# Six planner times and two copy engines changed in a sliding-window attention + gated MLP kernel

## The chip, the cores and the metric

The kernel runs on one core of one Trainium2 chip. The metric is the device time of one execution in microseconds (us), as the median of several runs. The profile shows one such execution. TensorE is called PE below (its weight loads PEld), VectorE DVE, ScalarE ACT, GpSimd POOL, SyncE SP.

## The reference

Eight batches `b` of eight heads, 576 positions, head size 64. Each query sees itself and the 63 keys before it. What follows is an MLP over 4608 rows of 512 columns with 2048 hidden columns, whose activation is `h * cos(h)`.

```python
scores = scale * np.matmul(q, k.transpose(0, 1, 3, 2))
mask = (rel >= 0) & (rel < window)          # window = 64
attn = softmax(np.where(mask, scores, -1e9))
x = np.matmul(attn, v).transpose(0, 2, 1, 3).reshape(B * S, H * D)
h = x @ w_in
out = (h * np.cos(h)) @ w_out
```

## The kernel before, in words

**Tiles.** The 4608 rows are cut into nine tiles `mt` of 512 rows, a batch into nine blocks `j` of 64 positions, the heads into four pairs `p`. A unit is one block of one pair: 64 queries against 128 keys, for two heads.

**The MLP of a tile.** PE makes `h_ps` in 16 blocks (`first`, L437; four matmuls each, one for each pair's quarter `ks` of xT), ACT takes the sine (L594), DVE multiplies (L597), and PE makes `out_ps` from the result (L609), 64 matmuls in four row groups. Each row group's `out_ps` is copied to `out_sb`, by DVE for even and by ACT for odd groups (L613). Before the 16 blocks `skewed` does the first three blocks by quarters, so that quarter 0 of xT is enough to begin with.

**Attention of batch b = t + 1** is done in the stage `t`, mostly among the output matmuls of tile `mt = t`. Units are put in groups of up to four, numbered here by `i` within the stage. A group goes through: scores on PE (`g_scores_across`, matmul L301), mask and maximum on DVE (`g_max`, L325, one instruction for each unit), exponentials with their sum on ACT (`g_exp`, L336), reciprocal on DVE (`g_inv`, L343), product on POOL (`g_norm`, L350; for the first three groups of stage 0 on DVE), and a transpose (`g_trans`). The transpose is a DMA on SP's queue (L362), except for the groups in `DIRECT` of stage 0 (i = 0 to 3, 8 and 9), where PE transposes (L359) and DVE copies the result (`g_put`). Then `values` multiplies with v on PE (L377) into `o_ps`, for the four pairs in turn, and `put_x` copies `o_ps` into xT (L113, the line of a helper that all copies share).

**Loads.** q, k and v of later batches are loaded by DMAs that POOL issues (`load_chunk`, L161, five chunks of 128 positions for q and five for k; `load_v`, L167). For batches from 2 on SP transposes q and k by DMA (`turn`, L246).

**What sets the order.** Nothing reorders at run time: each engine works its instructions in the order in which the code emits them. From stage 0's second half on, that order comes from a plan. `at(time, fn, ...)` (L461) books a step at a planner time; `pump(time)` (L464) emits all steps booked up to that time; the MLP loops call `pump` once after each `h_ps` block (planner time +1) and once after each four output matmuls (+1). A stage is `T = 32` planner units long, and its output matmuls begin at `Q = 16`. So a booked time says between which matmuls a step stands in PE's order, and where it stands on every other engine and queue. It says nothing of microseconds.

**Banks.** Scores go into PSUM banks by a list: in stage 0 two groups at a time over the banks X1, S, X0 in turn (L479); in later stages in two bursts, the groups i = 0 to 3 (banks t, t, t, X1) and, at i = 4, all others (t, t, t, S, X1, X0), L481. A bank is written again only when `g_max` has read it.

**The end of a stage.** The last group of a stage gets its reciprocal, product and transpose by times set from the stage's end (`lags`, L482: `T - 0.79`). The four `values` steps are booked at 1.01 before the next tile (L518), and the four copies into xT at 0.81, 0.71, 0.61 and 0.51 before it (L523). So DVE's order there is: copy of pair 0, the last reciprocal, copies of pairs 2 and 3; ACT copies pair 1.

Of the kernel before, what the change touches and what calls it, by code (L numbers as in the profile page):

```python
# [39 lines left out]
Q = 16  # L40
T = 2 * Q
LAGS = (0.2, 1, 3.2, 3.4, 3.8)
# [18 lines left out]
def kernel(  # L61
# [209 lines left out]
    groups = [[(0, p, j) for j in range(GF * g, GF * g + GF)] for p in range(PAIRS) for g in range(TU // GF)]  # L271
# [12 lines left out]
    direct = set(range(n_first)) | {n_first + i for i in DIRECT}  # L284
# [176 lines left out]
    def at(time, fn, *args):  # L461
        plan.append((time, len(plan), fn, args))
# [8 lines left out]
    ready = {(0, p, j): 0 for p in range(PAIRS) for j in range(TU)}  # L471
    n = n_first
    for t in range(B - 1):
        last = max(i for i, units in enumerate(groups) if units[0][0] == t + 1)
        time = T * t + Q - 1.4
        for i in range(last + 1 - n):
            time += PACE * len(groups[n - 1]) if i else 0
            if t == 0 and i % 2 == 0:
                at(time, g_scores_across, n, 2, (S_BANKS + S_BANKS)[i % 3:])  # L479
            elif t and i in (0, 4):  # L480
                at(time, g_scores_across, n, last + 1 - n if i else 4, "t t t S X1 X0".split() if i else "t t t X1".split())  # L481
            lags = LAGS[:2] + tuple(T * t + T - 0.79 - time + 0.01 * s for s in range(3)) if n == last and t else LAGS  # L482
            for lag, fn in zip(lags, (g_max, g_exp, g_inv, g_norm)):
                at(time + lag, fn, n, *("d" for _ in range(1) if fn is g_norm and n < n_first + 3))
            at(time + (4.6 if n in direct else lags[-1]), g_trans, n)
            if n in direct:
                at(time + 4.9, g_put, n)
            ready.update({unit: time + (5.9 if n in direct else 8.5) for unit in groups[n]})
            n += 1

    for b in range(1, B):
        t0 = T * (b - 1)
        if b == 1:
            for p in range(0, PAIRS, 2):
                for i, (tr, put) in enumerate(((tr_q, put_q), (tr_k, put_k))):
                    at(7 + 1.8 * (p + i), tr, b, p, p + 1)
                    for e, engine in enumerate("da"):
                        at(7.01 + 1.8 * (p + i) + 0.01 * e, put, b, p + e, engine)
        else:
            for i, name in enumerate(("q", "k")):  # L500
                for c in range(NC):
                    time = 4 + 0.5 * (c + NC * i) if b == 2 else t0 - T + 8 + 0.9 * (c + NC * i)
                    at(t0 - T + (22.1 if b == 2 else 18.5) + 1.44 * (c - 2) if i and c > 1 else time, load_chunk, name, b, c)
                for c, (lo, hi) in enumerate(((0, 2), (2, NC)) if i else ((0, NC),)):
                    at(t0 - (5.8 if b > 2 else 3.4) + 0.1 * i + 0.1 * c, turn, name, b, lo, hi)
            for c in range(5):
                at(t0 + 3.5 + 0.9 * c, load_v, b, c)
            for time, part in ((13.5, 0), (19.9, 2), (21.7, 3)):
                at(t0 + time, spread_v, b, part, None)
# [5 lines left out]
    for mt in range(1, n_mt):  # L515
        for p in range(PAIRS):
            time = max(ready[b, p - p % 2 + i // TU, j] for i in range(2 * TU) for b, j in (divmod(mt * TU + i % TU, NU),))
            time = max(time, 25.5) if mt == 1 else T * mt - (8.01 if mt == n_mt - 1 else 1.01)  # L518
            at(time, values, mt, p)
            if mt == 1:  # L520
                at(time + 0.3 + 0.2 * (p % 2), put_x, mt, p)
            else:
                at(time + 0.2 + 0.1 * p, put_x, mt, p, "a" if p == 1 else None)  # L523


    for name in ("q", "k"):
# [122 lines left out]
```

## Time and profile before

| | |
|---|---|
| median of 3 runs | 311.13 us (309.15, 311.13, 311.28) |
| the profiled execution's own time | 309.06 us |
| its span, first to last instruction | 307.1 us |
| PE busy | 292.3 us, 95% of the span |
| ACT busy | 235.6 us, 77% |
| DVE busy | 222.9 us, 73% |
| POOL busy | 170.3 us, 55% |

Times inside the profile run from the span's start. Stage 0's attention lies at about 41 to 60 us, and a later stage takes some 31 us: about 14 us of `h_ps` blocks, then about 17 us of output matmuls with the attention of the next batch. A timeline row has the start, the time from the first start to the last end of the merged instructions, the engine and line, the operation, the tiles written and read, and their count; what stands in square brackets is the idle time of the engine before the row, and what ended it. A matmul's row ends when its pipeline is empty, so the next matmul can begin before that end.

### The profile page before, as it was taken

How to read it: one execution, taken by the hardware profiler on the slowest of the kernel's cores; microseconds unless marked ns; L12 is line 12 of the kernel's file. 1: busy time of each engine (PE TensorE's matmuls, PEld its weight loads, DVE VectorE, ACT ScalarE, POOL GpSimd, SP SyncE). 2: the span in 40 equal slices, each digit the busy share in tenths (PEclk: the TensorE clock that was granted, in tenths of full speed). 3: DMA queues.
4: the chain of work that ended last, by engine and by line, in shares of the span. 5: the costliest groups of instructions: out<-in, count | busy, mean ns of one | idle time of the engine just before them, and what ended most of it. 6: DMA issues, size and time to landing. Idle time of an engine off the chain costs nothing.

```text
span 307.1 us, 8045 instructions
## 1 busy us (share of the span) xinstructions
PE 292.3 (95%) x2732; PEld 148.6 (48%) x2732; DVE 222.9 (73%) x841; ACT 235.6 (77%) x785; POOL 170.3 (55%) x204
## 2 busy tenths in 40 slices
PE   3979999899989989999989999999999999999996
PEld 2658854444444444444444545454544454454443
DVE  4866998778957896789867986798689768235801
ACT  4898799767997799779976998699869986116600
POOL 8997357793789376946895489648803620000000
PEclk9979999999999999999999999999999999999999
DMA  7999999999999999999999999999994342011011
GB/s 143 180 211 209 206 160 154 122 166 146 224 114 153 151 229 147 152 135 229 149 164 149 215 159 162 159 208 174 176 174 149 78 101 99 0 70 69 2 68 69
DMA packets 168921, 44.73 MB, mean 146 GB/s; under 512 B 158000, under 2 KB 164144, under 8 KB 168880
## 3 DMA queue, kind: packets, MB, share of 16 engines
q0 software_dynamic: 99344, 18.06, 82.6%
q1 hardware_dynamic: 69392, 25.96, 46.2%
q8 instruction: 21, 0.34, 0.5%
q10 hardware_dynamic: 144, 0.20, 0.2%
q14 instruction: 20, 0.16, 0.2%
HBM read 36.70 MB, written 9.44 MB: 150 GB/s over the span
## 4 chain that ended last, share of the span: by engine, by line
PE 57%; DVE 11%; DMA 9%; ACT 7%; POOL 6%; issue 5%; SPq 3%; DVEq 0%; POOLq 0%
PE h_ps L437 30%; PE out_ps L609 15%; DMA wT<-w 8%; DVE s L325 5%; PE h_ps L414 5%; ACT e L336 5%; POOL w L350 4%; SPq L246 2%; PE o_ps L377 2%; DMA q<-in_q_dram 2%; DVE v L113 2%; PE s_ps L301 1%; SPq L362 1%; PE out_ps L449 1%; POOL k L161 1%
## 5 line engine op out<-in xcount | busy, mean ns | idle before, releaser
L609 PE MATMUL out_ps<-w_out,gT 128*128 128x512 bf16 x560 | 125.2, 380 | 0.0
L437 PE MATMUL h_ps<-xT,w_in 128*128 128x512 bf16 x512 | 112.5, 379 | 0.6 <-ACT xT L113 0.5
L597 DVE TENSOR_TENSOR gT<-h_ps,sin 128x512 bf16<-128x512 f32 x128 | 84.8, 687 | 30.6 <-ACT sin L594 30.6
L350 POOL TENSOR_TENSOR w<-e,rden 128x512 bf16<-128x512 f32 (+1 forms) x76 | 72.0, 960 | 55.5 <-DVE rden L343 43.6
L336 ACT ACTIVATE e<-s,negm 128x128 f32<-128x128 f32 x256 | 98.6, 387 | 0.3 <-DVE negm L325 0.3
L594 ACT ACTIVATE sin<-h_ps 128x512 f32<-128x512 f32 x128 | 73.8, 599 | 31.5 <-PE h_ps L437 30.8
L609 PEld LDWEIGHTS <-gT 128*128 128x128 bf16 x560 | 53.0, 98 | 62.4
L437 PEld LDWEIGHTS <-w_in 128*128 128x128 bf16 x512 | 49.6, 98 | 60.2 <-issue 1.4
L325 DVE CUSTOM_DVE_ANT_0 s<-s_ps,mask 128x128 f32<-128x128 f32 x256 | 57.8, 280 | 1.7 <-PE s_ps L301 1.5
L336 ACT ACTIVATION_READ_ACCUMULATOR e<-s,negm 128x1 f32 x256 | 47.9, 187 | 0.0
L167 POOL DMA_DIRECT2D v<-in_v_dram x40 | 34.1, 873 | 1.0 <-DMA k<-in_k_dram 1.0
L161 POOL DMA_DIRECT2D k<-in_k_dram x30 | 26.4, 883 | 10.5 <-DMA v<-in_v_dram 9.0
L161 POOL DMA_DIRECT2D q<-in_q_dram x30 | 25.4, 883 | 10.0 <-DMA w_out<-in_moe_w_out_dram 8.6
L113 ACT COPY out_sb<-out_ps 128x512 f32<-128x512 f32 (+1 forms) x18 | 10.1, 562 | 26.1 <-PE out_ps L609 20.6
L113 DVE CAST xT<-o_ps 128x512 bf16<-128x512 f32 x26 | 16.9, 681 | 12.5 <-PE o_ps L377 11.0
L113 DVE COPY out_sb<-out_ps 128x512 f32<-128x512 f32 x18 | 12.2, 679 | 13.2 <-PE out_ps L609 13.2
L343 DVE RECIPROCAL rden<-den 128x4 f32<-128x4 f32 (+1 forms) x80 | 13.5, 171 | 10.6 <-ACT e L336 6.1
L325 DVE DVE_READ_ACCUMULATOR2_ANT negm<- 128x1 f32 x256 | 20.4, 80 | 0.0
L414 PE MATMUL h_ps<-xT,w_in 128*128 128x256 bf16 x128 | 16.4, 283 | 0.0
L113 DVE COPY v<-v 64x1024 bf16<-64x1024 bf16 (+1 forms) x19 | 15.7, 824 | 0.4
L414 PEld LDWEIGHTS <-w_in 128*128 128x128 bf16 x128 | 12.4, 102 | 1.8
L425 DVE TENSOR_TENSOR gT<-h_ps,sin 128x512 bf16<-128x512 f32 x16 | 10.8, 688 | 3.0 <-ACT sin L420 2.9
(60 smaller groups left out, 182.0 us busy)
## 6 DMA issues: line engine op xcount, KB each, us to landing
out_dram<-out_sb SPq DMA_DIRECT2D x16, 512.0 KB, 7.5
v<-in_v_dram POOLq DMA_DIRECT2D x32, 128.0 KB, 6.6
q<-in_q_dram POOLq DMA_DIRECT2D x24, 128.0 KB, 11.1
k<-in_k_dram POOLq DMA_DIRECT2D x24, 128.0 KB, 8.4
w_out<-in_moe_w_out_dram POOLq DMA_DIRECT2D x2, 1024.0 KB, 17.0
w_in<-in_moe_w_in_dram POOLq DMA_DIRECT2D x2, 768.0 KB, 11.1
wT<-w SPq DMA_TRANSPOSE x66, 5.7
out_dram<-out_sb SPq DMA_DIRECT2D x3, 256.0 KB, 2.0
```

What stands on the lines that cost most here:

```text
L113: {"a": nc.scalar.copy, "p": nc.gpsimd.tensor_copy}.get(engine, nc.vector.tensor_copy)(out, in_)
L161: nc.gpsimd.dma_start(out=st[name, b][:n, c].rearrange("p (h d) -> p h d", h=H), in_=src.rearrange("h p d -> p h d"))
L167: nc.gpsimd.dma_start(out=vt.rearrange("p (h d) -> p h d", h=H), in_=v[b, :, c * 128:c * 128 + n, :].rearrange("h p d -> p h d"))
L325: nc.vector.tensor_tensor_reduce(out=s[:, u], in0=s_ps[:, u], in1=mask[:, 2 - j % 2 if j else 0], scale=-scale if b else -1.0, scalar=BIG, ...
L336: nc.scalar.activation(e[:, u], s[:, u], AF.Exp, bias=negm[:, u:u + 1], scale=1.0 if n < n_first else -1.0, accum_out=den[:, u:u + 1])
L343: nc.vector.reciprocal(out=rden[:, 0:len(groups[n])], in_=den[:, 0:len(groups[n])])
L350: (nc.gpsimd if engine == "p" else nc.vector).tensor_tensor(out=w[:, 0:u], in0=e[:, 0:u], op=ALU.mult, in1=rden[:, 0:u].unsqueeze(2).to_br ...
L414: nc.tensor.matmul(out=st["h0", i][:, e], lhsT=w_in_sb[:, ks, ff * 128:ff * 128 + 128], rhs=st["xT", 0][:, ks, half], start=ks + e == 0, s ...
L437: nc.tensor.matmul(out=st["h", ff], lhsT=w_in_sb[:, ks, ff * 128:ff * 128 + 128], rhs=st["xT", mt][:, ks], start=start, stop=stop)
L594: nc.scalar.activation(sin, h_ps, AF.Sin, bias=math.pi / 2.0)
L597: nc.vector.tensor_tensor(out=gt[:, e], in0=h_ps, in1=sin, op=ALU.mult)
L609: nc.tensor.matmul(out=o_ps[e], lhsT=gT[ff // 2][:, ff % 2, ms * 128:ms * 128 + 128], rhs=w_out_sb[:, ff], start=ff == 0, stop=ff == n_ff - 1)
```

## The change

Four places change. (1) In stage 0, the PE transposes of group i = 3 are booked at +5.5 instead of +4.6, and their copy 0.3 behind them. (2) For batch 2, the loads of k chunks 2 and 3 are booked with those of chunks 0 and 1 (planner times 7.5 and 8.0 instead of 22.1 and 23.5), and chunk 4 at 26.9 instead of 25.0. (3) In the stages from 1 on, the second burst of scores is booked no earlier than `Q + 4.3` after the stage's begin; all later groups of the stage move with it. By the list of groups this moves a burst in stage 2 alone (by 1.4 units); elsewhere it lies at Q + 4.36 already. (4) At the end of the stages from 1 on, the last group's reciprocal, product and transpose are booked at `T - 0.65`, and ACT copies pair 2 of xT instead of pair 1.

In the emitted order this reads as follows. PE, stage 0: the 12 score matmuls of groups 8 and 9 and four output matmuls now stand ahead of the three transposes of group 3. DVE there: the reciprocal of group 5 and the mask steps of group 8 stand ahead of the copy of group 3. POOL there: four k loads in a row, the products of groups 3 to 7, the last k load, the other products. PE, stage 2: eight output matmuls ahead of the burst of 48 score matmuls. DVE and ACT there: the mask steps of group 4 stand behind a v copy and two reciprocals, and ACT copies `out_sb` behind group 4's exponentials instead of group 5's. At the ends of six stages DVE's order is: copies of pairs 0 and 1, the last reciprocal, copy of pair 3. SP in stage 2: the DMA transpose of group 6 stands behind the three DMA transposes of batch 4's q and k (`turn`) instead of ahead of them. No instruction is added or removed; elsewhere POOL's and SP's orders are the same.

```diff
+            if t and i == 4:
+                time = max(time, T * t + Q + 4.3)
...
-            lags = LAGS[:2] + tuple(T * t + T - 0.79 - time + 0.01 * s for s in range(3)) if n == last and t else LAGS
+            lags = LAGS[:2] + tuple(T * t + T - 0.65 - time + 0.01 * s for s in range(3)) if n == last and t else LAGS
...
-            at(time + (4.6 if n in direct else lags[-1]), g_trans, n)
+            lag = (5.5 if i == 3 else 4.6) if n in direct else lags[-1]
+            at(time + lag, g_trans, n)
             if n in direct:
-                at(time + 4.9, g_put, n)
-            ready.update({unit: time + (5.9 if n in direct else 8.5) for unit in groups[n]})
+                at(time + lag + 0.3, g_put, n)
+            ready.update({unit: time + (lag + 1.3 if n in direct else 8.5) for unit in groups[n]})
...
-                    at(t0 - T + (22.1 if b == 2 else 18.5) + 1.44 * (c - 2) if i and c > 1 else time, load_chunk, name, b, c)
+                    if i and c > (3 if b == 2 else 1):
+                        time = 26.9 if b == 2 else t0 - T + 18.5 + 1.44 * (c - 2)
+                    at(time, load_chunk, name, b, c)
...
-                at(time + 0.2 + 0.1 * p, put_x, mt, p, "a" if p == 1 else None)
+                at(time + 0.2 + 0.1 * p, put_x, mt, p, "a" if p == 2 else None)
```

## The prediction

> **What bounds the kernel now.** I read the page first: how busy the engines are, and the mean pace of PE.
>
> ```profile
> span 307.1 us, 8045 instructions
> PE 292.3 (95%) x2732; PEld 148.6 (48%) x2732; DVE 222.9 (73%) x841; ACT 235.6 (77%) x785; POOL 170.3 (55%) x204
> L437 PE MATMUL h_ps<-xT,w_in 128*128 128x512 bf16 x512 | 112.5, 379 | 0.6 <-ACT xT L113 0.5
> ```
>
> PE is the bound, with few gaps; the change removes no work, so it can gain only what PE waits. One row takes 379 ns from start to end, but 512 of them fill 112.5 us, so PE takes up a new one each 0.22 us. A waiting PE therefore loses some 0.16 us more than the idle time in brackets says, and I count each wait from the 0.22.
>
> Then the view of waits, PE's rows:
>
> ```profile
> PE tw_ps L359 <- POOL w L350: 2.8, 3, 1.1
> PE o_ps L377 <- DMA wT<-w: 2.2, 2, 1.2
> PE s_ps L301 <- DVE negm L325: 0.8, 1, 0.8
> PE h_ps L437 <- ACT xT L113: 0.5, 2, 0.2
> ```
>
> The columns are total, times, longest. Behind the start-up, these are about all of PE's waits. The edits are aimed at the first (of its three, two lie in stage 0's attention), the third and the fourth; the second, for DMA transposes, is touched by none, and it is where a wait may move to.
>
> **Edits 1 and 2, stage 0.** PE's timeline from 42 to 62 us, then POOL's, then two DVE rows:
>
> ```profile
> 48.36 1.03 PE L609 MATMUL out_ps<-w_out,gT 128*128 128x512 bf16 x4
> 50.13 0.34 PE L359 MATMUL tw_ps<-ident,w 128*128 128x128 bf16 x3 [0.74 <-POOL w L350]
> 50.40 0.36 PE L301 MATMUL s_ps<-kT,qT 64*64 64x128 bf16 x12
> 50.69 2.77 PE L609 MATMUL out_ps<-w_out,gT 128*128 128x512 bf16 x12
> 53.39 0.42 PE L301 MATMUL s_ps<-kT,qT 64*64 64x128 bf16 x16
> 53.74 1.90 PE L609 MATMUL out_ps<-w_out,gT 128*128 128x512 bf16 x8
> 56.68 0.34 PE L359 MATMUL tw_ps<-ident,w 128*128 128x128 bf16 x3 [1.04 <-POOL w L350]
> 57.81 0.70 PE L377 MATMUL o_ps<-wT,v 128*64 128x64 bf16 x32
> 60.22 0.70 PE L377 MATMUL o_ps<-wT,v 128*64 128x64 bf16 x32
> ```
>
> ```profile
> 45.35 1.79 POOL L161 DMA_DIRECT2D k<-in_k_dram  x2
> 49.25 0.82 POOL L350 TENSOR_TENSOR w<-e,rden 128x384 bf16<-128x384 f32 x1 [2.11 <-DVE negm L325]
> 50.98 0.84 POOL L350 TENSOR_TENSOR w<-e,rden 128x384 bf16<-128x384 f32 x1
> 51.75 0.94 POOL L161 DMA_DIRECT2D k<-in_k_dram  x1
> 53.49 0.73 POOL L161 DMA_DIRECT2D k<-in_k_dram  x1
> 54.23 3.19 POOL L350 TENSOR_TENSOR w<-e,rden 128x384 bf16<-128x384 f32 x4
> ```
>
> ```profile
> 49.39 0.28 DVE L325 CUSTOM_DVE_ANT_0 s<-s_ps,mask 128x128 f32<-128x128 f32 x1
> 54.69 0.17 DVE L343 RECIPROCAL rden<-den 128x3 f32<-128x3 f32 x1
> ```
>
> PE is through at 48.36 + 4 x 0.22 = 49.24 and starts group 3's transposes at 50.13: 0.89 lost. After the edit 12 score matmuls come first. They aren't free to go at once: group 9's bank X1 is still read by group 6's mask step (49.39 + 0.28 = 49.67). So PE goes on at 49.7; scores 0.29 (50.40 to 50.69), four output matmuls 0.88: transposes at 50.87, when the product (49.25 + 0.82 = 50.07) is long there. Transposes 0.27, eight output matmuls 1.76, scores 0.35, eight output matmuls 1.76: PE stands before group 8's transposes at 55.0. In the old run it stood there at 53.74 + 1.76 = 55.5 and got them at 56.68.
>
> Those waited for POOL, which came late with products because k loads stood between them. Now four k loads follow each other, 45.35 + 4 x 0.90 = 48.95, in POOL's 2.11 us of idle time, so group 3's product still starts at 49.25 (a cover of 0.3; each tenth beyond delays it by a tenth, and PE by nothing until 0.8). The products of groups 4 to 7 then follow DVE's reciprocals, the first by 51.0 instead of 51.8; the last k load (0.73) ends by 54.4. Group 8's reciprocal came at 54.69, 1.30 behind PE's scores at 53.39; now these start at 52.9, hence 54.2, end 54.4, product 0.80, transposes at 55.35. Gain: 56.68 - 55.35 = 1.33. Two waits of 0.89 + 1.18 become 0.46 + 0.35.
>
> What is late next are the DMA transposes for `values`. From SP's timeline, and the view of DMAs from 45 to 62 and from 66.7 to 68 us (median us from issue to landing at the end):
>
> ```profile
> 51.85 5.73 SPq L362 DMA_TRANSPOSE wT<-w  x4
> ```
>
> ```profile
> wT<-w SPq DMA_TRANSPOSE x4, 4.3
> ```
>
> ```profile
> wT<-w SPq DMA_TRANSPOSE x1, 8.9
> ```
>
> Now the fourth is issued at 51.85 + 5.73 - 1.2 = 56.4 and lands near 60.7 by the median, against the `o_ps` run from 60.22 that uses it in its second half, from 60.5: nothing to spare. After the edit the first is issued at 51.0 and SP needs about 1.25 for each, so the fourth at 54.75, 1.6 earlier; PE comes 1.33 earlier. So it holds if landing stays at 4.3. The low end is a landing 0.8 longer, gain 0.5; the high end 1.35. I take 1.3, as landing is nearest to the four of this same place.
>
> **Edit 3, stage 2.** PE's timeline from 104 to 124 us, and the view of wT at 119 us:
>
> ```profile
> 109.69 0.64 PE L301 MATMUL s_ps<-kX,qX 64*64 64x128 bf16 x32
> 111.17 0.42 PE L301 MATMUL s_ps<-kX,qX 64*64 64x128 bf16 x16 [0.84 <-DVE negm L325]
> 121.98 1.22 PE L377 MATMUL o_ps<-wT,v 128*64 128x64 bf16 x64
> ```
>
> ```profile
> L362 SPq DMA_TRANSPOSE wT<-w x1: 1190/1190/1190, 118.9 to 118.9; - x1
> ...
> DMA to landing us min/median/max: 3.8/3.8/3.8
> ```
>
> Eight output matmuls ahead of the burst bring PE there at 109.69 + 1.76 = 111.45, when X1 is free (111.17): the wait, 0.9, goes. But `o_ps` at 121.98 needs group 5's transpose for the last two blocks of pair 2, 0.61 + 0.23 in, at 122.8; it was issued at 118.9 and landed at 122.7. PE now comes 0.9 earlier and that transpose doesn't: group 5's mask steps and reciprocal stand behind the moved burst and a v copy, if anything 0.2 later. So the wait moves to `o_ps <- DMA wT`. Ends: 0.9 if the transpose lands early, -0.2 if it comes late by DVE's new order. I take 0.15, nearest to the landing row. SP's group 6 transpose, now behind three others, is needed a stage later: nothing.
>
> **Edit 4, stage ends.** Timelines from 182 to 190 and, PE, ACT and DVE, from 215.4 to 217.6 us and of PE from 200 to 220:
>
> ```profile
> 185.57 4.73 PE L437 MATMUL h_ps<-xT,w_in 128*128 128x512 bf16 x20
> 186.48 3.55 PEld L437 LDWEIGHTS <-w_in 128*128 128x128 bf16 x17 [0.36 <-issue]
> ```
>
> ```profile
> 216.24 0.81 PE L437 MATMUL h_ps<-xT,w_in 128*128 128x512 bf16 x3
> 216.49 1.25 DVE L113 CAST xT<-o_ps 128x512 bf16<-128x512 f32 x2
> 216.66 0.59 ACT L113 CAST xT<-o_ps 128x512 bf16<-128x512 f32 x1
> ```
>
> ```profile
> 217.29 2.96 PE L437 MATMUL h_ps<-xT,w_in 128*128 128x512 bf16 x13 [0.24 <-ACT xT L113]
> ```
>
> Three matmuls on quarter 0 last from 216.24 to 216.90; quarter 1 is copied by ACT, behind its last exponentials, until 217.25. Lost: 0.39, twice (the view of waits has two such). At 185.57 the weights for quarter 1 come at 186.48 instead of 186.23: 0.25. Sum 1.03. With the edit, DVE copies quarter 1 right behind quarter 0, 0.63 later (1.25 for two), done before 216.90; ACT's copy, quarter 2 now, is needed at 217.56 and is there at 217.25. Quarter 3 follows the last reciprocal (0.18) on DVE and is needed at 218.2. The other stage ends show no such wait. Ends: 0.5 (the bracketed time) and 1.03; I take 1.0. The last product starts up to 0.7 later, and POOL's v, q and k loads behind it. The cover is POOL's idle time ahead of the next stage's first product:
>
> ```profile
> 109.48 0.82 POOL L350 TENSOR_TENSOR w<-e,rden 128x384 bf16<-128x384 f32 x1 [3.86 <-DMA wT<-w]
> ```
>
> Without those 3.86, each tenth would delay that stage's transposes by a tenth.
>
> **Sum.** 1.3 + 0.15 + 1.0 = 2.45 us. The profiled execution took 309.06, 307.1 of it span: 306.6. It stands 2.07 below the median of 311.13; of the four executions known two lie near 309.1 and two near 311.2. I set the forecast in the middle, one above the sum: 307.6.
>
> **Rivals.** *The burst pays in full (0.22).* Group 5's transpose lands 0.75 earlier, because k loads and stores share the engines with it differently: another 0.75, 305.9 by the profiled execution. Against it: nothing releases that transpose sooner.
>
> *The gain of stage 0 is not carried on (0.2).* If transposes in stages 1 and 2 land when the DMA engines get round to them, whenever they were issued, PE waits at 91 or 122 us for what it gained: 1.3 lost, 307.9. For it: the two waits of 2.2 us for transposes. Against it: 3.8 at 119 us and 8.9 at 67 show that landing goes with what is in flight there, and that is issued earlier too.
>
> *Slower: the k loads slow the transposes (0.1).* Four k loads in a row put more loads beside the four transposes of stage 0. If these land in 8.9 us as at 67 us, the fourth lands at 54.75 + 8.9 = 63.65, while the old run used it at 60.5: 3.15 lost there, 1.15 gained elsewhere: 311.1. It decides from a landing of 4.3 + 0.15 + 1.3 + 1.15 = 6.9 us on. [...]
>
> **Chances.** My forecast 0.48, burst in full 0.22, not carried on 0.2, slower 0.1. The range goes from 309.06 - 1.35 - 0.9 - 1.03 = 305.8, less 0.4 of scatter, 305.4, to the third case in a higher execution, 307.9 + 2.07 = 310.0, and some of the fourth: 310.4. About 1%, 3.1 us, is what a measurement can tell here. The forecast's 2.45 is 0.8%: within. Faster by over 1%: the first rival (3.2 us) lies just beyond it, six in ten of its 0.22; of my own case a quarter of 0.48, with executions 2 us apart: 0.25. Slower by over 1%: half of the fourth case, which gives 2.0 us, and a little for the third in a higher execution: 0.08. Within: 0.67.
>
> **What would show it.** Right: no bracket on PE's transposes near 50 us and under 0.5 near 55; no bracket on the scores near 110; a new one of about 0.7, for wT, within `o_ps` near 121; none for xT at 216 and 247. Wrong: wT landing over 6 us in stage 0, a POOL product of group 3 starting later than the reciprocal, or `h_ps` waiting for DVE's copy of quarter 1 or ACT's of quarter 2.

## The result, and the profile after

The changed kernel takes 308.87 us in the median of 21 runs (306.18 to 311.16), the kernel before 310.45 us (308.72 to 311.58, 21 runs on the same chip). The ratio is 0.995, with a 95% interval of 0.9931 to 0.997: about 1.55 us less, where 2.45 had been predicted, and within the 1% that was forecast as likeliest. Here and below a median is that of all executions, while a ratio and its interval leave out the slow ones, those over 1.5% above the fastest of the same kernel. The execution that was profiled is the longest of the 21 (311.16 us), so its stages can be read one by one, but not its length.

The head of the page of the kernel after:

```profile
span 309.1 us, 8044 instructions
PE 293.9 (95%) x2732; PEld 149.8 (48%) x2732; DVE 222.2 (72%) x841; ACT 235.9 (76%) x785; POOL 170.8 (55%) x204
PEclk9979999999988999999999999999999999999999
```

The view of waits of the kernel after, PE's rows behind the start-up (total, times, longest):

```profile
PE o_ps L377 <- DMA wT<-w: 5.4, 4, 2.3
PE tw_ps L359 <- POOL w L350: 1.2, 2, 1.0
PE s_ps L301 <- DVE negm L325: 0.2, 1, 0.2
```

The three waits that the edits aim at behave as they should: `tw_ps` for POOL's product has fallen from 2.8 to 1.2 (1.0 of it lies ahead of stage 0's attention, where nothing was changed), the scores' wait from 0.8 to 0.2, and the row for xT, 0.5 before, is gone. The fourth wait, which no edit touches, has grown from 2.2 to 5.4 us. The clock row has a second dip, in the 12th and 13th slice.

**Stage 0.** PE's timeline of the kernel after, then POOL's, then the view of DMAs from 45 to 62 us, then SP's timeline and one of its rows by itself (the 2382 are the ns for which SP was at it):

```profile
42.17 0.36 PE L301 MATMUL s_ps<-kT,qT 64*64 64x128 bf16 x12
...
49.58 0.36 PE L301 MATMUL s_ps<-kT,qT 64*64 64x128 bf16 x10 [0.17 <-DVE negm L325]
...
50.74 0.33 PE L359 MATMUL tw_ps<-ident,w 128*128 128x128 bf16 x3
...
55.23 0.34 PE L359 MATMUL tw_ps<-ident,w 128*128 128x128 bf16 x3 [0.26 <-POOL w L350]
...
58.88 1.09 PE L377 MATMUL o_ps<-wT,v 128*64 128x64 bf16 x32
59.91 4.27 PE L437 MATMUL h_ps<-xT,w_in 128*128 128x512 bf16 x19
```

```profile
45.50 3.54 POOL L161 DMA_DIRECT2D k<-in_k_dram  x4
49.10 4.37 POOL L350 TENSOR_TENSOR w<-e,rden 128x384 bf16<-128x384 f32 x5
```

```profile
wT<-w SPq DMA_TRANSPOSE x4, 4.6
```

```profile
50.87 6.65 SPq L362 DMA_TRANSPOSE wT<-w  x4
...
L362 SPq DMA_TRANSPOSE wT<-w x1: 2382/2382/2382, 53.8 to 53.8; - x1
```

Group 3's transposes start at 50.74 without a wait, group 8's at 55.23 after 0.26, and the second `o_ps` run at 58.88 instead of 60.22: 1.34 us earlier. The four k loads end at 49.04, and group 3's product follows at 49.10. But that second `o_ps` run takes 1.09 instead of 0.70. SP issued the first transpose at 50.87, as forecast, and was then held by the third for 2.38 us, so the fourth was issued at 56.3, no earlier than before (56.4). It landed 3.2 later, at 59.5, when PE was already in the run. The `h_ps` block behind the run starts at 59.91; in the kernel before it starts at 60.85:

```profile
42.33 0.36 PE L301 MATMUL s_ps<-kT,qT 64*64 64x128 bf16 x12
...
60.85 1.47 PE L437 MATMUL h_ps<-xT,w_in 128*128 128x512 bf16 x6
```

So 0.94 is left at the end of stage 0. Of this 0.16 is older than the edits, since PE is already that much earlier at the 12 score matmuls near 42 us. Counted from these matmuls, stage 0 takes 17.74 us instead of 18.52, a gain of 0.78.

**Where more of it is lost.** PE's timeline of the kernel after from 86 to 110 us, then the clock in windows there (busy times of the engines, granted clock, share of the DMA engines, GB/s):

```profile
88.46 0.38 PE L377 MATMUL o_ps<-wT,v 128*64 128x64 bf16 x12
91.16 1.60 PE L377 MATMUL o_ps<-wT,v 128*64 128x64 bf16 x52 [2.32 <-DMA wT<-w]
92.69 14.79 PE L437 MATMUL h_ps<-xT,w_in 128*128 128x512 bf16 x64
107.41 0.53 PE L301 MATMUL s_ps<-kX,qX 64*64 64x128 bf16 x24
```

```profile
88.00:92.00 4.00, 1.68 (x48) 1.17 (x48) 0.66 (x2) 2.20 (x11) 1.65 (x3) 0.87 1.43 208
92.00:94.00 2.00, 2.00 (x33) 1.11 (x28) 1.48 (x4) 1.62 (x2) 1.04 (x2) 0.50 0.96 180
94.00:96.00 2.00, 2.00 (x10) 0.88 (x9) 0.00 (x0) 0.39 (x2) 2.00 (x3) 0.91 1.14 137
```

The same place in the kernel before:

```profile
89.40 0.38 PE L377 MATMUL o_ps<-wT,v 128*64 128x64 bf16 x12
90.72 1.09 PE L377 MATMUL o_ps<-wT,v 128*64 128x64 bf16 x52 [0.95 <-DMA wT<-w]
91.76 13.98 PE L437 MATMUL h_ps<-xT,w_in 128*128 128x512 bf16 x64
105.67 0.53 PE L301 MATMUL s_ps<-kX,qX 64*64 64x128 bf16 x24
```

PE comes to `o_ps` the 0.94 of stage 0 earlier (88.46 against 89.40) and leaves the next `h_ps` blocks 1.74 later (107.41 against 105.67). The transpose that it waits for was issued 0.9 earlier too (86.6 against 87.5), but landed after 4.5 us instead of 3.2. In between lie 1.37 more of wait (2.32 - 0.95), and then a time at half clock, in which 52 `o_ps` matmuls take 0.51 longer (1.60 - 1.09) and 64 `h_ps` matmuls 0.81 longer (14.79 - 13.98). These three are 2.69 = 0.94 + 1.74 but for rounding. The windows give the length of the half clock: (1 - 0.87) x 4 / 0.5 + 2.0 + (1 - 0.91) x 2 / 0.5 = 1.04 + 2.0 + 0.36 = 3.4 us. In the profile before the clock is at 1.00 all through this stretch, with its wait of 0.95. Two later waits for wT are longer than before as well: 1.61 instead of 1.21 near 155 us, and 1.19 and 0.32 near 218 us, where the kernel before had none.

### The profile page after: what moved, and what is told of

It is laid out like the page before. It is cut to its first block, busy times and chain, and to the rows that moved or that the text cites. A ratio compares the mean times of both kernels' runs of the same rounds, so it can differ in the third digit from the quotient of the medians.

```text
span 309.1 us, 8044 instructions
## 1 busy us (share of the span) xinstructions
PE 293.9 (95%) x2732; PEld 149.8 (48%) x2732; DVE 222.2 (72%) x841; ACT 235.9 (76%) x785; POOL 170.8 (55%) x204
## 4 chain that ended last, share of the span: by engine, by line
PE 74%; DMA 9%; ACT 5%; DVE 4%; POOL 4%; issue 2%; POOLq 0%; DVEq 0%
PE h_ps L437 36%; PE out_ps L614 24%; DMA wT<-w 8%; PE h_ps L414 5%; ACT e L336 4%; PE o_ps L377 3%; POOL w L350 2%; PE s_ps L301 2%; DVE s L325 2%; DMA q<-in_q_dram 1%; PE out_ps L449 1%; PE tw_ps L359 1%; ACT L429 1%; PE tq_ps L210 1%; DVE v L113 1%
## 5 line engine op out<-in xcount | busy, mean ns | idle before, releaser
L602 DVE TENSOR_TENSOR gT<-h_ps,sin 128x512 bf16<-128x512 f32 x128 | 84.8, 687 | 32.5 <-ACT sin L599 32.5
L437 PEld LDWEIGHTS <-w_in 128*128 128x128 bf16 x512 | 49.8, 98 | 59.7 <-issue 1.1
L377 PE MATMUL o_ps<-wT,v 128*64 128x64 bf16 x512 | 12.0, 202 | 5.6 <-DMA wT<-w 5.4
L113 DVE COPY v<-v 64x1024 bf16<-64x1024 bf16 (+1 forms) x19 | 14.9, 786 | 0.4
L377 PEld LDWEIGHTS <-v 128*64 128x64 bf16 x512 | 10.3, 116 | 10.0 <-issue 9.8
```

Of the source, the lines that this page charges most:

```text
L113: {"a": nc.scalar.copy, "p": nc.gpsimd.tensor_copy}.get(engine, nc.vector.tensor_copy)(out, in_)
L377: nc.tensor.matmul(out=o_ps[64 * h:64 * h + 64, 64 * i:64 * i + 64], lhsT=vtiles[b % 2][:, max(j - 1, 0), 128 * p + 64 * h:128 * p + 64 * ...
L437: nc.tensor.matmul(out=st["h", ff], lhsT=w_in_sb[:, ks, ff * 128:ff * 128 + 128], rhs=st["xT", mt][:, ks], start=start, stop=stop)
L602: nc.vector.tensor_tensor(out=gt[:, e], in0=h_ps, in1=sin, op=ALU.mult)
```

## The experiments

Theory A: each edit gives PE what the prediction says, and the sum arrives. Theory B: each edit gives PE that much, but PE then comes earlier to `o_ps`, which waits for DMA transposes that land late; what is won is partly handed back there. The rivals within B are what makes the landing late: the loads in flight, SP's queue, or the stores.

### Each edit alone, and edits 1, 2 and 4 together

Edits 1 and 2 alone:

```diff
+            lag = (5.5 if i == 3 else 4.6) if n in direct else lags[-1]
+            at(time + lag, g_trans, n)
...
+                    if i and c > (3 if b == 2 else 1):
+                        time = 26.9 if b == 2 else t0 - T + 18.5 + 1.44 * (c - 2)
```

> Edits 1 and 2 alone (stage 0: group 3's transposes later, k chunks 2 and 3 earlier). Theory A (the prediction): PE's second o_ps run of stage 0 begins 1.3 us earlier than before (60.2 to about 58.9), the transposes of stage 1 are issued as much earlier, and 1.3 us are gained in all. Theory B (landing): the transposes that values needs at the end of stage 1 land when the DMA engines get to them; then the wait of PE on wT near 91 us grows from 0.95 to about 2 and under 0.5 us are left.

Measured: 309.59 us (308.24 to 315.1, 12 runs), ratio 0.9983, interval 0.9945 to 1.0021.

Edit 3 alone:

```diff
+            if t and i == 4:
+                time = max(time, T * t + Q + 4.3)
```

> Edit 3 alone (burst of stage 2 behind eight more output matmuls). Theory A (the prediction): the wait of the scores on negm near 111 us (0.8 in brackets) is gone, and about 0.7 of it comes back as a wait within o_ps on wT near 121; gain 0.15. Rival (pays in full): no wait at 121, gain 0.9.

Measured: 309.75 us (307.91 to 313.41, 12 runs), ratio 0.9985, interval 0.9956 to 1.0015.

Edit 4 alone:

```diff
-            lags = LAGS[:2] + tuple(T * t + T - 0.79 - time + 0.01 * s for s in range(3)) if n == last and t else LAGS
+            lags = LAGS[:2] + tuple(T * t + T - 0.65 - time + 0.01 * s for s in range(3)) if n == last and t else LAGS
...
-                at(time + 0.2 + 0.1 * p, put_x, mt, p, "a" if p == 1 else None)
+                at(time + 0.2 + 0.1 * p, put_x, mt, p, "a" if p == 2 else None)
```

> Edit 4 alone (ACT copies pair 2 of xT, DVE pairs 0, 1 and 3, last reciprocal later). Theory A (the prediction): h_ps has no wait on xT at 186, 217 and 248 us, gain 1.0. Theory B (landing): PE comes earlier to the next stage's end, but the transposes don't land earlier; a wait on wT appears there and under 0.5 is left.

Measured: 308.93 us (306.95 to 311.92, 12 runs), ratio 0.9961, interval 0.9925 to 0.9997.

Edits 1, 2 and 4, the first and the third diff together:

> Edits 1, 2 and 4, without the burst. Theory A: 2.3 us faster than before, 0.15 slower than the whole change. Theory B (landing): between 0.5 and 1.5 faster, with waits on wT of over 2 us more in sum than before. Rival (burst pays in full): 0.9 slower than the whole change.

Measured: 308.23 us (306.23 to 308.89, 7 runs), ratio 0.9911, interval 0.9879 to 0.9944. The kernel before took 310.24 us in these comparisons (30 runs).

PE's row for wT in the view of waits of each: edits 1 and 2 alone, then edit 3 alone, then edit 4 alone:

```profile
PE o_ps L377 <- DMA wT<-w: 4.4, 4, 2.2
```

```profile
PE o_ps L377 <- DMA wT<-w: 4.2, 6, 1.0
```

```profile
PE o_ps L377 <- DMA wT<-w: 1.3, 2, 1.0
```

Edit 3 alone, PE's timeline:

```profile
111.50 0.86 PE L301 MATMUL s_ps<-kX,qX 64*64 64x128 bf16 x48
...
122.46 0.74 PE L377 MATMUL o_ps<-wT,v 128*64 128x64 bf16 x32 [1.05 <-DMA wT<-w]
123.51 0.51 PE L377 MATMUL o_ps<-wT,v 128*64 128x64 bf16 x20 [0.32 <-DMA wT<-w]
```

What follows: with edit 3 alone the burst has no wait any more, and 1.37 us of waiting stand within `o_ps` near 123 us, where the kernel before had none. Edits 1 and 2 alone bring o_ps's wait from 2.2 to 4.4, 2.18 of it near 91 us, as theory B expected. Edit 4 alone has 1.3 and no wait for xT, as theory A expected. The gains alone are worth about 0.5, 0.5 and 1.2 us, each with some 1 us on either side, so of the single edits only the fourth's gain is clear of zero. Edits 1, 2 and 4 together gain 2.8 us with 2.5 us of waits, where theory A expected 2.3, and theory B 0.5 to 1.5 with over 2 us more of waits than the 2.2 of the kernel before. Theory B missed there.

### The whole change, and the same with few bytes to load

The whole change again:

> The changed kernel once more, for a second profile and beside the others of this call. Theory A: the PE side of all four edits is there (no wait near 50, 111, 217 and 248 us beyond 0.3), 2 to 3 us faster, and what is missing is chance. Theory B (landing): 1.5 us faster, and the waits of o_ps on wT sum to over 3 us (2.2 in the profile of before). Theory C (burst harms in company): slower than edits 1, 2 and 4 alone, which had a ratio of 0.991, by 1 us.

Measured: 310.19 us (307.09 to 315.16, 12 runs), ratio 0.998, interval 0.9946 to 1.0015.

Then the kernel before and the kernel after, each with the q and k loads of batches 3 to 7 cut to one head of eight (their other rows aren't loaded, so those batches' scores are not the reference's):

```diff
-        nc.gpsimd.memset(rows[name][b % 2].rearrange("p (c x) -> p c x", c=NC)[64:128, NC - 1], 0.0)
+        nc.gpsimd.memset(rows[name][b % 2].rearrange("p (c x) -> p c x", c=NC)[64 if b < 3 else 0:128, NC - 1], 0.0)
...
+        nh = H if b < 3 else 1
-        nc.gpsimd.dma_start(out=st[name, b][:n, c].rearrange("p (h d) -> p h d", h=H),
-                            in_=src.rearrange("h p d -> p h d"))
+        nc.gpsimd.dma_start(out=st[name, b][:n, c].rearrange("p (h d) -> p h d", h=H)[:, 0:nh],
+                            in_=src.rearrange("h p d -> p h d")[:, 0:nh])
```

> The kernel before, with the q and k loads of batches 3 to 7 cut to one head of eight (the other seven heads' scores are then computed from old rows, so the output is another). Same instructions, an eighth of those loads' bytes. Theory B (landing is set by what else the DMA engines carry): transposes land in 3 to 5 us, the waits of o_ps on wT (2.2 us) go, and it is about 2 us faster. If landing is set by the transposes themselves: no difference over 0.5 us.

Measured: 307.22 us (306.3 to 308.78, 8 runs), ratio to the kernel before 0.9913, interval 0.9879 to 0.9947.

> The same cut in the changed kernel (other output for the same reason). Theory B: no waits on wT either, so the difference to the thin kernel before is what the four edits give PE by themselves: 1.3 + 0.9 + 1.0 = 3.2 us, against 1.5 with full loads. If the edits give PE less than that: the difference stays near 1.5.

Measured: 304.34 us (303.86 to 305.04, 5 runs), ratio to the kernel before 0.9823, interval 0.979 to 0.9856.

PE's timeline of the whole change again, near 121 us, and its wT row in the view of waits:

```profile
110.25 0.86 PE L301 MATMUL s_ps<-kX,qX 64*64 64x128 bf16 x48
...
120.63 0.74 PE L377 MATMUL o_ps<-wT,v 128*64 128x64 bf16 x32 [0.47 <-DMA wT<-w]
121.98 0.51 PE L377 MATMUL o_ps<-wT,v 128*64 128x64 bf16 x20 [0.61 <-DMA wT<-w]
```

```profile
PE o_ps L377 <- DMA wT<-w: 5.4, 7, 2.4
```

The changed kernel with few bytes to load, its view of waits and its DMAs:

```profile
PE o_ps L378 <- DMA wT<-w: 0.9, 2, 0.5
```

```profile
wT<-w SPq DMA_TRANSPOSE x66, 3.1
```

And how long the transposes took to land that were issued from 84 to 92 us, ahead of the wait at 91 us: kernel before, kernel after, kernel after with few bytes:

```profile
DMA to landing us min/median/max: 2.5/2.8/4.3
```

```profile
DMA to landing us min/median/max: 3.7/4.7/6.5
```

```profile
DMA to landing us min/median/max: 2.4/2.4/2.5
```

What follows: without most of those bytes the same edits are worth 307.22 - 304.34 = 2.9 us, and the waits on wT stay under 1 us. With them, the median landing of all 66 transposes is 6.3 us in the profile after and 5.7 in that before, and the waits take 5.4 us. So behind stage 0 the landing of the transposes beside the loads takes part of the gain back: theory B. The median landing alone doesn't set the waits, though: with edit 3 alone it is 5.0, and the waits take 4.2.

The 2.9 us are near the 3.2 expected, but not by the parts expected. In the two profiles with few bytes stage 0 gives 0.5, stage 1 0.3, stage 2 0.8 and all behind it 1.3. Stage 0's own loads, those of batch 2, are not cut, and it doesn't give its 1.3 there either. Edit 4 has more to take away, since the kernel before with few bytes waits four times for xT, 1.8 us in all, where the profile of before has 0.5.

The whole change again, at 0.998, gained less than theories A and B expected, and by the ratio it is some 2 us slower than edits 1, 2 and 4 alone, where theory C expected 1. Its waits are those of theory B. The wait of edit 3 stands where the prediction put it, near 121 us, with 0.47 + 0.61; in the profile after it is missing, and the part on stage 2 below says what goes with that.

### A try at a remedy: the stores on ACT's queue

Edits 1, 2 and 4, with the stores taken off SP's queue and booked earlier:

```diff
-        nc.sync.dma_start(out=out[r0:r0 + n * 128].rearrange("(a p) f -> p a f", p=128), in_=o_sb[:, e:e + n])
+        queue = nc.sync if mt == n_mt - 1 else nc.scalar
+        queue.dma_start(out=out[r0:r0 + n * 128].rearrange("(a p) f -> p a f", p=128), in_=o_sb[:, e:e + n])
...
-                at(base + T + 6 + ms0 / 2, store, o_sb, mt, ms0, 0, 2)
+                at(base + T + 1.2 + ms0, store, o_sb, mt, ms0, 0, 2)
```

> Edits 1, 2 and 4 without the burst, and the output stores issued from ACT's queue after the first sines of the next tile, some 8 to 10 us earlier than SP does it behind the stage's last transposes. Theory B: stores no longer run beside the first transposes of the next stage; these land in 4 to 5 us instead of 6 to 8, and it gains 0.5 to 1.5 us on the kernel with edits 1, 2 and 4. If stores don't matter: the same as that, ratio 0.991; slower if they hold up the q and k transposes that the next scores need.

Measured: 322.14 us (316.82 to 324.97, 6 runs), ratio 1.0273, interval 1.0212 to 1.0334. The transposes did land sooner (4.8 us in the median) and PE waited 2.0 us for them, but DVE has a new row in the view of waits, and v's loads land later:

```profile
DVE v L113 <- DMA v<-in_v_dram: 16.1, 5, 4.4
```

```profile
v<-in_v_dram POOLq DMA_DIRECT2D x32, 128.0 KB, 8.5
```

What follows: v's loads took 6.6 us before and take 8.5; the copies of v stand on DVE ahead of the mask steps, so a late v holds up the scores of a whole stage (PE waits 6.6 us for the mask steps and 6.0 for gT). The transposes won and v's loads lost, which have less slack here. Whether the stores' other queue or their earlier time did it wasn't told apart.

### Side by side: with and without the burst, with and without early k loads

Edits 1, 2 and 4 and the whole change once more, and both with the k loads of batches from 3 on booked in one row, where POOL is idle:

```diff
-                    if i and c > (3 if b == 2 else 1):
-                        time = 26.9 if b == 2 else t0 - T + 18.5 + 1.44 * (c - 2)
+                    if i and c > 3 and b == 2:
+                        time = 26.9
```

> Edits 1, 2 and 4 without the moved burst, a second time, beside the whole change on the same chip. Theory B (what the edits win at TensorE is taken back where o_ps waits for DMA transposes that land late, and the moved burst adds such a wait at 121 us and nothing else): a ratio of 0.991 to 0.994 to the kernel before, the whole change 0.994 to 0.997, so 0.5 to 1 us apart. Rival (the first measurement of this kernel was a lucky one, the burst is worth its 0.15 us): 0.995, and the whole change the same or 0.15 us better.

Measured: 307.88 us (306.8 to 309.62, 12 runs), ratio 0.9934, interval 0.9904 to 0.9964.

> The whole change. Theory B: ratio 0.995 to 0.997, waits of o_ps on wT of 4 to 5.5 us in all, with one of 0.5 to 1.1 near 121 us. Rival (the burst pays): at or below the ratio of the kernel without it in this call.

Measured: 308.46 us (306.75 to 312.55, 12 runs), ratio 0.9954, interval 0.9916 to 0.9991.

> Edits 1, 2 and 4, and from batch 3 on the last three k loads are booked behind the first two (planner times 14.3 to 16.1 of the stage), where POOL is idle for 4.6 us, and no longer between the first products. Theory B: the late transposes no longer share the DMA engines with these loads, and the first products come 1 to 2.6 us earlier; waits of o_ps on wT fall from 2.5 us to under 1, 1 to 1.5 us less than without it: 306.8 to 307.2, ratio 0.988 to 0.989. Rival (the loads' place does not matter, only their number): the same as without it, 308.2, ratio 0.991. Against both: the k loads now lie beside those of v and q, which may land later and hold up the DMA transposes of q and k: over 309.

Measured: 311.8 us (309.6 to 316.2, 12 runs), ratio 1.0038, interval 1.0002 to 1.0073.

> The whole change with the same k loads moved. Theory B: group 5's transpose in stage 2 is no longer beside the k loads of batch 4 and its product comes earlier, so the burst's 0.9 us are kept: no wait on wT over 0.3 us near 121 us, 0.7 to 0.9 us faster than the kernel without the burst: 306.0 to 306.4, ratio 0.985 to 0.987. Rival (group 5 comes late because of DVE's order, not of loads): the wait of about 0.7 near 121 us stays, and the time is that of the kernel without the burst.

Measured: 306.92 us (305.39 to 312.79, 6 runs), ratio 0.9888, interval 0.9832 to 0.9944. The kernel before took 309.95 us here (29 runs).

PE's timeline of edits 1, 2 and 4 with early k loads, in stages 1 and 4, and the DMA transposes issued from 175 to 183 us:

```profile
89.44 0.51 PE L377 MATMUL o_ps<-wT,v 128*64 128x64 bf16 x20 [0.39 <-DMA wT<-w]
...
182.85 0.44 PE L377 MATMUL o_ps<-wT,v 128*64 128x64 bf16 x16 [0.55 <-DMA wT<-w]
184.86 0.46 PE L377 MATMUL o_ps<-wT,v 128*64 128x64 bf16 x16 [1.57 <-DMA wT<-w]
186.44 0.28 PE L377 MATMUL o_ps<-wT,v 128*64 128x64 bf16 x6 [1.12 <-DMA wT<-w]
```

```profile
wT<-w SPq DMA_TRANSPOSE x5, 8.1
```

What follows: theory B's stronger form, that the place of these loads decides, fell: edits 1, 2 and 4 with early k loads were to take 306.8 to 307.2, and took 311.8. At 89 us the wait did shrink (0.39), but at 183 to 186 us there are three, 3.24 us in all, because transposes land in 8.1 us there. The profile of the whole change with early loads, its longest execution, has the same three (0.60, 1.48 and 1.46), and near 121 us it waits 0.55 and 0.31, where theory B expected none over 0.3; three others of its executions took 305.39 to 305.96. It has the lowest median of all kernels with the full computation, 306.92, on six runs over 7.4 us; edits 1, 2 and 4 as they are come to 307.88 and 308.23, with at most 2.8 us between their runs. Which of the two is the better kernel is not settled. Edits 1, 2 and 4 the second time have the ratio that theory B expected (0.9934). The whole change the third time has it too (0.9954), but no wait near 121 us, and 6.3 us of waits on wT in all where 4 to 5.5 were expected.

### What the burst is worth: stage 2 in all profiles

Stage 2 can be timed by itself in every profile, from its first scores to the first `h_ps` block behind its `o_ps`. The rows for the kernel after, PE's timeline (there is no wait near 123 us):

```profile
107.41 0.53 PE L301 MATMUL s_ps<-kX,qX 64*64 64x128 bf16 x24
...
122.69 1.20 PE L377 MATMUL o_ps<-wT,v 128*64 128x64 bf16 x64
123.92 5.34 PE L437 MATMUL h_ps<-xT,w_in 128*128 128x512 bf16 x24
```

That is 123.92 - 107.41 = 16.51 us. The same from the other profiles:

| kernel | first scores at | stage 2 |
|---|---|---|
| before | 105.67 | 17.54 |
| edits 1 and 2; edit 4; 1, 2 and 4 (two profiles) | 104.40 to 107.62 | 17.54 or 17.55 each |
| edits 1, 2, 4, early k loads | 103.79 | 18.24 |
| few bytes, before | 104.35 | 17.54 |
| few bytes, after | 103.98 | 16.76 |
| the whole change: the profile after, and the third | 107.41, 109.78 | 16.51 each |
| the whole change again | 104.50 | 17.92 |
| the whole change, early k loads | 104.59 | 17.69 |
| edit 3 alone | 105.75 | 18.20 |

With its old place the burst gives 17.54 unless the transposes are late. With the new place stage 2 takes 16.51, 1.03 less, where they are in time, and 0.15 to 0.66 more than 17.54 where they are late. The two profiles of the whole change with 16.51 are those in which PE had just lost a wait of 2.32 or 4.15 us and the half clock behind it and came to stage 2 at 107.4 us or later, which would give the transfers more time; the transposes issued from 113 to 121.5 us landed there in 2.4 to 5.3 us, and in 3.6 to 5.8 us in the whole change again:

```profile
DMA to landing us min/median/max: 2.4/3.2/5.3
```

```profile
DMA to landing us min/median/max: 3.6/3.6/5.8
```

So the burst paid in full where PE came to stage 2 after such a loss, and 0.78 of it with few bytes to load. It cost some tenths where PE came at 104.5 to 105.75, with the other edits and alone.

**Stage 0 by the same measure.** Stage 0 can be timed in the same way, from the 12 score matmuls near 42 us to the `h_ps` block behind the second `o_ps` run:

| kernel | 12 scores at | stage 0 | landing of its four transposes, median |
|---|---|---|---|
| without edits 1 and 2 (four profiles) | 41.22 to 42.42 | 18.52 to 18.71 | 3.9 to 4.4 |
| edits 1 and 2; the whole change, third | 42.66, 42.68 | 17.45, 17.47 | 4.8 each |
| the whole change: the profile after, and with early k loads | 42.17, 42.37 | 17.74, 17.64 | 4.6 each |
| edits 1, 2, 4; the whole change again; few bytes, after | 41.75, 41.53, 41.64 | 18.24, 18.15, 18.18 | 5.4, 5.3, 5.4 |
| edits 1, 2, 4: early k loads, stores on ACT's queue | 41.32, 40.96 | 18.29, 18.44 | 5.4, 5.1 |
| edits 1, 2, 4, second time | 40.60 | 18.98 | 5.6 |

With the edits stage 0 ends at 59.4 to 60.2 us, whenever PE began it. Where PE began it late the edits gain 1.07, and where it began it early they lose 0.46, because `o_ps` waits for the transposes instead. PE's timeline of the last row, whose first transposes were issued at 49.7 and landed 6.6 later:

```profile
56.34 0.65 PE L377 MATMUL o_ps<-wT,v 128*64 128x64 bf16 x24 [1.22 <-DMA wT<-w]
```

On average over the ten profiles with the edits 0.5 us of the forecast 1.3 are left at the end of stage 0. That is also what edits 1 and 2 gained alone. The transposes land later with the edits in all ten, so it isn't only that PE comes earlier to them; whether the four k loads in a row or the earlier issue does it was not told apart.

### The executions by their clock

Each execution's mean granted clock is known. It is 0.994 in the profile before, which has one dip, that of the start-up, and 0.989 in that after, which has two; 1.00 is an execution without a dip. In the three sets of comparisons the kernel before ran 78 times: 22 executions near 1.00 took 309.4 us in the mean, 48 near 0.994 took 310.2, and 8 at 0.989 or less took 312.3. The one dip of a profile at 0.994 isn't always that of the start-up: in the whole change again and in edits 1, 2 and 4 with early k loads the clock is at 1.00 from 15 to 23 us, and by the windows the dip begins near 186 us in the one and 187.5 us in the other, at waits for wT that ended at 186.15 and 186.44 us. So the share at 0.989 or less tells of late transposes, but only roughly:

| kernel | executions | at 0.989 or less |
|---|---|---|
| before | 78 | 8 |
| edits 1 and 2 | 12 | 3 |
| edit 3 | 12 | 2 |
| edit 4 | 12 | 4 |
| edits 1, 2, 4 | 19 | 1 |
| the whole change: the result, again, third | 21, 12, 12 | 3, 7, 3 |
| edits 1, 2, 4, early k loads | 12 | 6 |
| few bytes, before and after | 13 | 0 |

The dips are not what is missing from the predicted 2.45. At the same clock the 45 executions of the whole change took 307.8, 308.8 and 310.8 us in the mean, 1.6, 1.5 and 1.6 less than the kernel before in its 78. So the shortfall of 0.9 is there without any dip, and the 0.8 that stage 0 didn't give (0.5 instead of 1.3) is about as much; that these two are the same is an estimate. What the dips do is to widen the spread: they hold the means of all executions, 309.1 and 310.2, to 1.1 apart.

## Why the prediction was right, and where it was off

- **Class and sign: right.** 2.45 us forecast, about 1.55 measured (0.9 to 2.1 by the interval), within 1%; the forecast time of 307.6 is 1.3 below the median, within its range.
- **Edits 1 and 2, 1.3 us: right for PE's waits, mis-sized for the stage.** The bank's release (49.58, predicted 49.7), the four k loads (ended 49.04, predicted 48.95) and group 8's transposes (55.23, predicted 55.35) came to a tenth or so, and the second `o_ps` run came 1.34 earlier. The step that failed is the one after it: "SP needs about 1.25 for each, so the fourth at 54.75", and "it holds if landing stays at 4.3". In the profile after, SP was held for 2.38 us by the third, the fourth was issued at 56.3, and the run took 0.4 longer; over ten profiles the landing is 4.6 to 5.6 in the median, and 0.5 us of the 1.3 are left at the end of stage 0. Alone these edits gave 0.5 us. The rival *not carried on* comes nearest, but it put the loss at 91 or 122 us: the first loss is in stage 0 itself, and the wait near 91 us grew only in three of the six profiles that have these edits and change no other load or store (2.18, 2.32 and 4.15; it was 0.93 to 0.95 in the other three).
- **Edit 3, 0.15 us: right in mechanism, with too narrow ends.** The wait went at 110 us and came back near 121 us for group 5's transpose, as 1.08 us in the whole change again and 1.37 alone. Between the ends of 0.9 and -0.2 the prediction took 0.15; stage 2 shows +1.03 in two profiles and -0.15 to -0.66 in three. "PE now comes 0.9 earlier and that transpose doesn't" thus holds in some executions and the rival *burst pays in full* in others, and 0.15 is a middle that no profile shows.
- **Edit 4, 1.0 us: right, as a figure for one execution.** No wait of `h_ps` for xT is left in the profile after; alone 1.2 us, with 0.1 to 2.3 in the interval. The wait that it takes away differs between profiles without it, in the view of waits: 0.5 in two places before, 1.4 in three with edit 3 alone, 0.5 in one with edits 1 and 2 alone, where other stage ends wait for wT instead.
- **The rival for slower, the k loads slowing stage 0's transposes: wrong there.** These landed in 4.6 us, and it needed 6.9. The half of it that held is the direction: 4.6 to 5.6 in all profiles with the edits, 3.9 to 4.4 in those without.
- **A term left out: the clock.** The prediction priced a wait at its length. The wait of 2.32 us near 91 us cost PE another 0.51 + 0.81 = 1.3 us behind it.
- **Luck in the total.** The forecast came within its range with its largest term at less than half its size, and with 0.15 for a term that was 1.03 in some executions and negative in others.
- **Still open.** The whole change was measured three times at 0.995, 0.998 and 0.9954, and without the burst twice at 0.9911 and 0.9934. In the one set that has both the burst takes 0.6 us, and the intervals overlap; across the sets it is 0.5 to 2.1. Stage 2 accounts for 0.4 of it (17.92 against 17.54), and the greater share at 0.989 for some more. With early k loads it is the other way round (306.92 against 311.8), of which stage 2 explains only 0.55 (18.24 - 17.69). What decides between an early and a late landing in a given execution was not found: not the place of the k loads alone, and the try with the stores changed two things at once. SP's queue, the third rival within theory B, was not varied, though SP held single transposes for 2.4 us in stage 0.

## What to carry to other kernels

When a bound engine is freed from one wait, look for the next thing that it needs and when that lands: here the DMA transposes of stage 0 had no slack, and of 1.3 us freed at PE 0.5 were left at the end of that stage. When an issue time is forecast for a transfer, ask what can hold the queue itself: SP's fourth transpose was forecast 1.6 us earlier and came no earlier, since the third held SP for 2.38 us. Gains that end in a transfer should be forecast as a spread over executions, since a landing of 4.5 or of 3.2 us at one place decided them here, and the wait of 2.32 us that the late one opened at PE was paid for twice, by the wait and by 1.3 us at half clock behind it. An edit that moves a wait to the next transfer was worth 1.03 us where PE was late by other waits and, with all bytes to load, less than nothing where it wasn't, so its gain isn't to be added to that of edits that make the engine earlier.

## What the runs showed of the hardware that was not expected

- In the profile after, PE's clock was granted at 0.50 from 19.27 to 22.68 us and from 90.95 to 94.36 us, 3.41 us each time, and at 1.00 between the two and from there to 309 us. In that before it was 0.50 from 19.27 to 22.68 us alone.
- The second of these stretches began 0.2 us before the wait of 2.32 us ended. In three other profiles the windows at a single long wait for wT and behind it give 3.4 us at half clock as well: 2.18 us (edits 1 and 2 alone, a clock of 0.57 from 91 to 95 us), 2.36 us (the whole change again, 0.95 from 184 to 186 us and 0.60 from 186 to 190) and 4.15 us (the whole change the third time, 0.65 from 93 to 97 us and 0.93 from 97 to 101).
- The length of a single wait isn't what decides. Three waits of 0.55, 1.57 and 1.12 us close together (edits 1, 2 and 4 with early k loads, 183 to 186 us) were followed by 3.4 us at half clock too (0.92 from 185 to 188 us, 0.64 from 188 to 192). The wait of 1.61 us near 155 us in the profile after was not. Nor was one of 2.27 us that ended at 151.75 us with the stores on ACT's queue: the nine output matmuls behind it took 2.12 us, at the pace of eight in 1.90 in the profile before. What decides was not shown.
- DMA transposes landed in 3.1 us in the median of 66 with one eighth of the q and k bytes of batches 3 to 7 to load, and in 5.0 to 6.4 us with all of them, though the transposes themselves are the same (the stores at another time on ACT's queue gave 4.8).
